# Sketched attention into a top-1 mixture of experts: rows of a tile fetched by a plain transfer on SP's queue, tasks in a new order

## The chip, the cores and the metric

One Trainium2 chip, one of its cores. The metric is the device time of one execution in microseconds (us); lower is better. A core has five engines that run their own instruction queues: TensorE (PE in the profile, with its weight loads as PEld), VectorE (DVE), ScalarE (ACT), GpSimd (POOL) and SyncE (SP). Transfers between memory and SBUF are issued from SP, ACT or POOL.

## The reference

```python
def _attn_ref(q, k, v, S1, S2):            # q, k, v: (4, 4, 1088, 32)
    def phi(x):                            # 64 features of a row
        a = np.einsum('rd,bhsd->bhsr', S1, x)
        b = np.einsum('rd,bhsd->bhsr', S2, x)
        return np.einsum('bhsi,bhsj->bhsij', a, b).reshape(*x.shape[:-1], r * r)
    q_p, k_p = (phi(q), phi(k))
    kv = np.einsum('bhsf,bhsd->bhfd', k_p, v)
    z = np.sum(k_p, axis=2)
    num = np.einsum('bhsf,bhfd->bhsd', q_p, kv)
    den = np.einsum('bhsf,bhf->bhs', q_p, z)[..., None] + 1e-06
    return num / den

def _moe_ref(x, w_gate, w1, w2):           # x: (4352, 128), 8 experts, F = 1024
    logits = x @ w_gate
    expert_idx = np.argmax(logits, axis=1)
    probs = softmax(logits)
    gate_w = probs[np.arange(N), expert_idx]
    for e in range(E):
        mask = expert_idx == e
        out[mask] = gate_w[mask, None] * (np.maximum(x[mask] @ w1[e], 0.0) @ w2[e])
```

The result of the attention, its heads side by side, is the `x` of the mixture: 4352 tokens of 128 numbers, each of which goes through one of eight experts.

## The kernel before

The kernel has two halves that overlap. **Attention** goes by the four batches (`b`) in two chunks of 512 rows (`c`) and a remainder of 64 rows, two batches' remainders together (`r`). Task names in `ORDER` (lines 50 to 58) carry these numbers: `T.Kbc` turns a chunk of keys on PE, `P.Kbc` projects it and makes the features, `V.Kbc` adds to the key-value state, `E.b` and `B.b` finish that state, `T.Q`, `P.Q`, `U.Q`, `N.Q` do the same for queries and divide. A name with `kr` or `qr` is a remainder. `A.b` copies a batch's values beside a column of ones (POOL), `L` issues the last batch's loads and the 16 loads of expert weights (SP).

**Routing** of a batch: `C.b` picks the expert (DVE), `G.b` takes the exponentials (ACT), `R.b` ranks the tokens within their experts with matmuls (PE, DVE), and `S.b` scatters the batch's rows into `xs_dram` in HBM, 128 rows to an indirect transfer of POOL (line 515): 8 or 9 transfers for a batch, 34 in all. An expert has `NTOK` rows of room in `xs_dram`; a row is 128 numbers, the gate weight and the token's number (`XW` = 130 words of 4 bytes).

**Experts** go by tiles of 128 rows of one expert. Up to `JT` = 41 tiles exist: 34 that always run (`JMIN`) and seven more in three optional groups of 4, 2 and 1, which run inside `tc.If` blocks (lines 808 to 821). Which expert and which rows a tile has is worked out by `table()` on DVE: the first table (tasks `W.i`) covers the first ten tiles (`JE`), full tiles of the tokens of batches 0 and 1 alone; the second covers the rest, once batch 3 is ranked, and its steps are called in the loop for tiles 5 and 6 (line 832). A tile goes through:

- `F.j` = `gather(j)` (line 691): an indirect transfer of POOL that fetches 128 rows by a list of 128 row numbers, `grow`, one of each partition; a number out of bounds fetches nothing
- `I.j` = `x_in(j)` (line 700): transpose on PE (line 703), copy on ACT, a register load and a copy of the expert's first weights on DVE (lines 706, 709)
- `Y.j` = `up(j)` (line 720): 16 matmuls (line 724), relu on ACT and DVE
- `Z.j` = `rows_out(j)` and `down(j)` (lines 711, 733): 16 matmuls (line 740), scaling on ACT; the list `to` of the tokens' numbers, of which `inv_i` makes the invalid ones out of bounds
- `store(j)` (line 745): an indirect transfer of POOL that writes 128 rows of the output

`Y` and `Z` are called half tiles in the text below. `ORDER` is written out by hand or by a program ahead of time; under the manual schedule each engine runs its instructions in the order in which the tasks issue them, and semaphores are set by the framework. After `ORDER` a loop (line 794) goes on with tile 5: it turns tile j + 2, does `up` of j + 1 and `down` of j, and then issues gathers `AHEAD` = 6 tiles ahead, one gather of an optional tile while there are any, and stores:

```python
        for i in range(JE, j + AHEAD + 1) if j == 6 else [j + AHEAD] if j > 6 else []:
            if i < JMIN:
                gather(i)
        if j > 6 and optional:
            gather(optional.pop(0))
        for _ in range(0 if j < 6 else j % 2 if optional else 2 if j + 1 < JMIN else JT):
            if waiting:
                store(waiting.pop(0))
```

Gathers rotate through 10 buffers, the optional tiles have seven of their own. Loads of the attention's inputs and of weights are issued on SP's queue from line 154 on, in the order in which they stand.

Of the kernel before, what the change touches and what calls it, by code (L numbers as in the profile page):

```python
# [32 lines left out]
FP = mybir.dt.float32  # L34
# [16 lines left out]
finish_s T.K00 T.K01 P.K00 P.K01 T.K11 T.K10 T.kr0 V.K00 P.kr0 D P.K11 P.K10 T.Q00 T.Q01 L T.Q11  # L51
V.K01 P.Q01 E.0 P.Q00 B.0 P.Q11 T.qr0 U.Q01 U.Q00 T.K21 T.Q10 N.Q00 P.qr0 N.Q01 C.0 P.Q10 P.K21
V.K10 V.K11 T.kr1 G.0 T.K20 R.0 U.qr0 U.Q11 E.1 P.K20 B.1 A.2 U.Q10 T.Q20 N.qr0 N.Q10 N.Q11 V.K20
V.K21 C.1 P.Q20 P.kr1 G.1 T.K31 T.Q21 A.3 R.1 T.K30 W.0 U.Q20 P.Q21 P.K30 P.K31 E.2 W.1 T.Q30 W.2
T.Q31 T.qr1 W.3 U.Q21 S.0 P.Q31 B.2 W.4 P.Q30 V.K30 S.1 N.Q21 N.Q20 V.K31 P.qr1 W.5 F.0 W.6 E.3 C.2
U.Q30 B.3 F.1 F.2 U.qr1 U.Q31 F.3 N.qr1 F.4 N.Q30 G.2 I.0 F.5 N.Q31 I.1 R.2 Y.0 I.2 I.3 C.3 Y.1 Z.0
I.4 Y.2 Z.1 F.6 G.3 S.2a I.5 S.2b R.3 Y.3 Y.4 S.3a S.3b Z.2 F.7 Y.5 Z.3 F.8 Z.4 I.6 F.9
# [4 lines left out]
def kernel(  # L62
# [12 lines left out]
    nc = tc.nc  # L75
# [60 lines left out]
    main = {}  # L136

# [28 lines left out]
    load_rem(lambda b: q_rem[:, b // 2], q, nc.sync, 0)  # L166
    load_main("k", k, 2)
# [284 lines left out]
    xs_dram = dram.tile([E * NTOK, XW], I32, name="xs_dram")  # L452

# [76 lines left out]

    tiles = {}
    done = const.tile([128, E], FP, name="done")

    def table(g, n, j0):
# [30 lines left out]
        if g:  # L565
# [36 lines left out]
        gr = tj("grow", I32, const)  # L602
        iv = None
# [9 lines left out]
        nc.vector.tensor_scalar(loc, loc, 128.0, iota_p, ALU.mult, ALU.add)  # L613
        if g:
# [179 lines left out]
    for j in range(sum(name[0] == "Z" for name in begun), JMIN):  # L794
# [28 lines left out]
        else:  # L823
# [52 lines left out]
```

## Time and profile before

| | us |
|---|---|
| median of 3 runs (283.54 to 286.17) | 283.83 |
| the profiled execution | 284.85 |
| its span in the trace | 282.7 |
| PE busy | 231.8 |
| POOL busy | 134.2 |
| DVE busy | 108.5 |
| ACT busy | 75.4 |

The profiled execution is 2.15 us longer than its span, since something lies around the span. Busy times are sums over instructions; matmuls are pipelined and their ends are modelled, so a busy PE is not PE at its peak. Idle time of an engine is put down to whatever released the next instruction; "issue" means that the profile shows nothing that it waited for. The granted clock (PEclk) is a share of 2.4 GHz.

### The profile page before, as it was taken

The page shows a single profiled execution, that of the slowest core. Times are in us where ns is not written, and L with a number is a line of the kernel's source. Part 1 is how long each engine was busy: PE and PEld are TensorE (multiplying, and loading weights), DVE is VectorE, ACT ScalarE, POOL GpSimd, SP SyncE. Part 2 cuts the span into 40 slices and gives each one's busy share as a digit, 9 for nine tenths or more (in the row PEclk, how much of TensorE's full clock was granted, in tenths as well). Part 3 has the DMA queues.
Part 4 walks back from the last instruction along what each step waited for, and adds up shares of the span by engine and source line. Part 5 has one row for each costly group of instructions (what it writes and reads, how often), then busy time and mean ns, then how long its engine had stood idle before and what let it go on. Part 6 is the DMA issues. An engine that isn't in the chain of part 4 may idle for free.

```text
span 282.7 us, 6720 instructions
## 1 busy us (share of the span) xinstructions
PE 231.8 (82%) x2558; PEld 216.2 (76%) x2558; DVE 108.5 (38%) x303; ACT 75.4 (27%) x198; POOL 134.2 (47%) x165
## 2 busy tenths in 40 slices
PE   8989875957975959669939559887887999999993
PEld 7989764836954949539939349787777998999993
DVE  4656735515844805410641012324323234224320
ACT  2555420404340305013200012221212232333321
POOL 5520373273072564740057747667576156263223
PEclk9999997975996886957977758999997999999999
DMA  6969999211011010110002111111110001010000
GB/s 196 286 191 361 367 377 376 84 47 31 2 40 28 30 48 20 59 38 0 2 21 56 36 38 33 50 35 44 33 48 26 17 21 44 14 37 21 20 9 21
DMA packets 23009, 22.69 MB, mean 80 GB/s; under 512 B 5844, under 2 KB 20184, under 8 KB 22976
## 3 DMA queue, kind: packets, MB, share of 16 engines
q1 hardware_dynamic: 18160, 14.95, 16.3%
q0 software_dynamic: 3712, 7.15, 8.6%
q8 instruction: 23, 0.38, 0.6%
q10 hardware_dynamic: 1104, 0.13, 0.3%
q14 instruction: 10, 0.08, 0.1%
HBM read 17.81 MB, written 4.95 MB: 81 GB/s over the span
## 4 chain that ended last, share of the span: by engine, by line
PE 65%; issue 19%; another core or an unknown queue 6%; ACT 3%; DMA 2%; POOL 2%; DVE 1%; POOLq 1%; ACTq 0%; DVEq 0%
PE ph L724 23%; PE py L740 18%; PE kv L342 4%; PE ab_K L319 4%; PE qp_Q L405 3%; PE nd_Q L417 3%; PE ab_Q L319 3%; PE idle L179 2%; PE tp_Q L310 1%; PE xgTp L703 1%; DMA out_dram<-y,to 1%; PE tp_K L310 1%; ACT q_pT_Q L408 1%; POOL out_dram L747 1%
## 5 line engine op out<-in xcount | busy, mean ns | idle before, releaser
L740 PE MATMUL py<-w_all,hT 128*128 x592 | 81.5, 290 | 9.9 <-issue 6.7
L724 PE MATMUL ph<-xgT,w 128*128 128x128 f32 x592 | 83.6, 295 | 7.3 <-issue 5.2
L724 PEld LDWEIGHTS ph<-xgT,w 128*128 128x128 f32 x592 | 77.7, 209 | 12.1 <-issue 9.9
L740 PEld LDWEIGHTS py<-w_all,hT 128*128 128x128 f32 x592 | 75.9, 205 | 12.8 <-issue 10.1
L692 POOL DMA_INDIRECT x_rows<-xs_dram,grow x41 | 42.9, 1047 | 48.4 <-issue 28.2
L731 DVE TENSOR_SCALAR hT<-ph 128x512 f32<-128x512 f32 x30 | 20.7, 691 | 101.6 <-ACT hT L726 70.0
L747 POOL DMA_INDIRECT out_dram<-y,to x34 | 35.0, 1031 | 43.3 <-ACT xgT L705 28.4
L515 POOL DMA_INDIRECT xs_dram<-x_rows,row_i x34 | 36.3, 1067 | 31.9 <-DVE base_e L509 9.5
L726 ACT ACTIVATE hT<-ph 128x512 f32<-128x512 f32 x37 | 22.2, 599 | 73.2 <-PE ph L724 36.9
L709 DVE COPY w<-w_all 128x1024 f32 x38 | 26.4, 704 | 20.7 <-remote 16.6
L743 ACT ACTIVATE y<-py,x_rows 128x128 f32<-128x128 f32 x34 | 12.5, 368 | 60.3 <-remote 27.6
L417 PE MATMUL nd_Q<-kvx,q_pT_Q 128*64 128x82 f32 x256 | 13.0, 244 | 7.0 <-issue 5.7
L703 PE MATMUL xgTp<-ident,x_rows 128*128 128x128 f32 x38 | 10.5, 298 | 7.8 <-DMA x_rows<-xs_dram,grow 4.4
L417 PEld LDWEIGHTS nd_Q<-kvx,q_pT_Q 128*64 128x64 f32 x256 | 10.8, 141 | 7.6 <-issue 5.6
L319 PE MATMUL ab_K<-s_cat,xT_K 128*64 128x64 f32 x256 | 12.0, 233 | 4.8 <-issue 4.4
L327 DVE TENSOR_TENSOR k_p<-half_K 128x1024 f32<-128x1024 f32 x8 | 10.5, 1328 | 11.7 <-issue 6.1
L319 PEld LDWEIGHTS ab_K<-s_cat,xT_K 128*64 128x64 f32 x256 | 9.7, 144 | 6.7 <-issue 6.3
L705 ACT COPY xgT<-xgTp 128x128 f32<-128x128 f32 x38 | 9.5, 265 | 15.3 <-remote 8.0
L327 DVE TENSOR_TENSOR q_p_Q<-half_Q 128x1024 f32<-128x1024 f32 x8 | 10.4, 1324 | 8.1 <-ACT half_Q L326 8.1
L342 PEld LDWEIGHTS kv<-k_p,v_aug 128*33 128x33 f32 x256 | 9.0, 125 | 4.1 <-issue 4.1
L342 PE MATMUL kv<-k_p,v_aug 128*33 128x64 f32 x256 | 10.4, 239 | 1.9 <-issue 1.9
L703 PEld LDWEIGHTS xgTp<-ident,x_rows 128*128 128x128 f32 x38 | 5.5, 149 | 7.5 <-issue 7.2
(164 smaller groups left out, 193.4 us busy)
## 6 DMA issues: line engine op xcount, KB each, us to landing
w_all<-in_moe_w_dram SPq DMA_DIRECT2D x16, 512.0 KB
k<-in_k_dram SPq DMA_DIRECT2D x4, 512.0 KB
v<-in_v_dram SPq DMA_DIRECT2D x4, 512.0 KB
q<-in_q_dram SPq DMA_DIRECT2D x4, 512.0 KB
x_rows<-xs_dram,grow POOLq DMA_INDIRECT x41
xs_dram<-x_rows,row_i POOLq DMA_INDIRECT x34
out_dram<-y,to POOLq DMA_INDIRECT x34
q_rem<-in_q_dram SPq DMA_DIRECT2D x4, 32.0 KB
```

The lines of the kernel that those rows point to most:

```text
L319: nc.tensor.matmul(ab[ts(m, 64)].rearrange("p (g i r) -> p g i r", g=4, i=n)[:, :, i], lhsT=st["xT"][:, ds(i * 128 + m * 64, 64)], rhs=s_c ...
L327: nc.vector.tensor_tensor(f.rearrange("p g (a b) -> p g a b", a=R), half[:, :, 0:R, None].broadcast_to(shape), half[:, :, None, R:2 * R].b ...
L342: nc.tensor.matmul(kv[b][g * RR:g * RR + DA, ts(n, RR)], lhsT=v1[:, h], rhs=k_p[:, h], start=(first and n == 0), stop=last, skip_group_che ...
L417: nc.tensor.matmul(nd[ts(m, 64), i, ds(hp * 2 * KC, 2 * KC)], lhsT=t[:, ds((i * NP + hp) * 128 + m * 64, 64)], rhs=kvx[bs[m]][:, hp].rearr ...
L515: d = nc.gpsimd.indirect_dma_start(out=xs_dram[:], out_offset=bass.IndirectOffsetOnAxis(ap=row_i[:, u:u + 1], axis=0), in_=x[:, u, :].bitc ...
L692: d = nc.gpsimd.indirect_dma_start(out=xg_of(j).bitcast(I32), out_offset=None, in_=xs_dram[:], in_offset=bass.IndirectOffsetOnAxis(ap=tile ...
L709: nc.vector.tensor_copy(out=w1, in_=w1_all[:, ds(wo, F)])
L724: nc.tensor.matmul(ph[:, ts(c, 128)], lhsT=w1[:, ts(c, 128)], rhs=xT, start=True, stop=True)
L726: nc.scalar.activation(hT[:, 0:512], ph[:, 0:512], AF.Relu)
L731: nc.vector.tensor_scalar(hT[:, 512:1024], ph[:, 512:1024], 0.0, None, ALU.max)
L740: nc.tensor.matmul(py[:, :DM], lhsT=hT[:, ts(c, 128)], rhs=w2_all[:, ds(wo + c * DM, DM)], start=(c == 0), stop=(c == NFC - 1))
L747: d = nc.gpsimd.indirect_dma_start(out=out[:], out_offset=bass.IndirectOffsetOnAxis(ap=to_of(j), axis=0), in_=y, in_offset=None, bounds_ch ...
```

## The change

A tile's rows are taken as 128 consecutive rows from one row number. The number comes out of the table as one value per tile (`first_row`), is loaded into a register of SP, and a plain transfer of SP's queue fetches the rows. An expert's last tile, which would reach past the expert's rows, is shifted back so that it ends with them (`min(of - 128, loc)`), and rows that belong to the tile before are marked invalid for the store, as are rows past the end of an expert with fewer than 128 rows in all. For the latter case the first 128 rows of each expert's room in `xs_dram` are filled with zeros, by one transfer on SP's queue ahead of the loads of batch 2. Optional tiles that don't run get tile numbers beyond the last tile. The tasks stand in a new order, and in the loop up to two stores are issued for each tile from tile 5 on. The declaration of `xs_dram`, of `zeros` and of `parts` moves up.

```diff
 ORDER = """
-finish_s T.K00 T.K01 P.K00 P.K01 T.K11 T.K10 T.kr0 V.K00 P.kr0 D P.K11 P.K10 T.Q00 T.Q01 L T.Q11
-V.K01 P.Q01 E.0 P.Q00 B.0 P.Q11 T.qr0 U.Q01 U.Q00 T.K21 T.Q10 N.Q00 P.qr0 N.Q01 C.0 P.Q10 P.K21
-V.K10 V.K11 T.kr1 G.0 T.K20 R.0 U.qr0 U.Q11 E.1 P.K20 B.1 A.2 U.Q10 T.Q20 N.qr0 N.Q10 N.Q11 V.K20
-V.K21 C.1 P.Q20 P.kr1 G.1 T.K31 T.Q21 A.3 R.1 T.K30 W.0 U.Q20 P.Q21 P.K30 P.K31 E.2 W.1 T.Q30 W.2
-T.Q31 T.qr1 W.3 U.Q21 S.0 P.Q31 B.2 W.4 P.Q30 V.K30 S.1 N.Q21 N.Q20 V.K31 P.qr1 W.5 F.0 W.6 E.3 C.2
-U.Q30 B.3 F.1 F.2 U.qr1 U.Q31 F.3 N.qr1 F.4 N.Q30 G.2 I.0 F.5 N.Q31 I.1 R.2 Y.0 I.2 I.3 C.3 Y.1 Z.0
-I.4 Y.2 Z.1 F.6 G.3 S.2a I.5 S.2b R.3 Y.3 Y.4 S.3a S.3b Z.2 F.7 Y.5 Z.3 F.8 Z.4 I.6 F.9
+finish_s T.K00 T.K01 P.K00 P.K01 T.kr0 T.K11 T.K10 P.kr0 D V.K00 P.K10 P.K11 T.Q01 T.Q00 L T.Q11 V.K01 P.Q00
+E.0 P.Q01 B.0 P.Q11 T.qr0 U.Q00 U.Q01 T.Q10 T.K21 N.Q00 P.qr0 P.Q10 N.Q01 V.K10 C.0 P.K21 G.0 V.K11 U.Q10
+T.K20 T.kr1 R.0 U.Q11 E.1 P.K20 U.qr0 B.1 T.Q20 N.qr0 A.3 N.Q11 N.Q10 C.1 A.2 P.Q20 P.kr1 G.1 V.K20 T.K31
+S.0 T.K30 T.Q21 R.1 W.0 V.K21 U.Q20 P.K31 E.2 P.Q21 W.1 P.K30 B.2 T.Q31 W.2 S.1 W.3 T.Q30 U.Q21 T.qr1 N.Q20
+N.Q21 V.K30 P.qr1 W.4 P.Q30 V.K31 W.5 P.Q31 F.0 E.3 U.qr1 U.Q30 B.3 F.1 F.2 F.3 C.2 G.2 U.Q31 N.Q30 I.0
+N.Q31 I.1 F.4 R.2 F.5 S.2a Y.0 I.2 S.2b F.6 F.7 N.qr1 C.3 I.3 Y.1 G.3 Z.0 Y.2 I.4 Y.3 Z.1 Y.4 R.3 F.8 Z.2
+S.3a I.5 Z.3 Z.4 W.6 S.3b Y.5 F.9 I.6
 """
...
     load_rem(lambda b: q_rem[:, b // 2], q, nc.sync, 0)
+    nc.sync.dma_start(out=xs_dram.rearrange("(e r) c -> r e c", e=E)[0:128],
+                      in_=zeros[:, None, :].bitcast(I32).broadcast_to([128, E, XW]))
     load_main("k", k, 2)
...
             begin = t1("begin", I32)
-            for i, (run, below) in enumerate(((4, 0), (2, 4), (1, 6))):
-                if i:
-                    nc.vector.tensor_scalar(begin[:, i:i + 1], bits[:, 0:1], below, None, ALU.bitwise_and)
+            nc.vector.memset(begin[:, 0:1], 0)
+            for i, below in (1, 4), (2, 6):
+                nc.vector.tensor_scalar(begin[:, i:i + 1], bits[:, 0:1], below, None, ALU.bitwise_and)
...
             begin_f = t1("begin_f")
-            nc.vector.tensor_copy(out=begin_f[:, 1:3], in_=begin[:, 1:3])
+            nc.vector.tensor_scalar(begin_f[:, 0:3], bits, 0, float(JT), ALU.is_equal, ALU.mult)
+            nc.vector.tensor_tensor(begin_f[:, 0:3], begin_f[:, 0:3], begin[:, 0:3], ALU.add)
             jn = tj("jn")
-            nc.vector.tensor_copy(out=jn, in_=jio[:, 0:n])
             base = JMIN - JE
-            nc.vector.tensor_scalar(jn[:, base + 4:base + 6], jio[:, base:base + 2], begin_f[:, 1:2], None, ALU.add)
-            nc.vector.tensor_scalar(jn[:, base + 6:base + 7], jio[:, base:base + 1], begin_f[:, 2:3], None, ALU.add)
+            nc.vector.tensor_copy(out=jn[:, 0:base], in_=jio[:, 0:base])
+            for i, tiles_here in enumerate(parts):
+                a, m = tiles_here[0] - JE, len(tiles_here)
+                nc.vector.tensor_scalar(jn[:, a:a + m], jio[:, base:base + m], begin_f[:, i:i + 1], None, ALU.add)
             yield
...
-        nc.vector.tensor_scalar(loc, loc, 128.0, iota_p, ALU.mult, ALU.add)
+        nc.vector.tensor_scalar(loc, loc, 128.0, None, ALU.mult)
         if g:
...
             nc.vector.tensor_scalar(of, of, cnt[:, 0:1], None, ALU.add)
-            inv = tj("inv")
-            nc.vector.tensor_tensor(inv, loc, of, ALU.is_ge)
+            begin = tj("begin_row")
+            nc.vector.scalar_tensor_tensor(begin, of, -128.0, loc, ALU.add, ALU.min)
+            nc.vector.tensor_scalar(begin, begin, 0.0, None, ALU.max)
+            nc.vector.scalar_tensor_tensor(first, ej, float(NTOK), begin, ALU.mult, ALU.add)
+
+            nc.vector.tensor_scalar(begin, begin, iota_p, None, ALU.add)
+            nc.vector.tensor_tensor(loc, begin, loc, ALU.is_lt)
+            nc.vector.tensor_tensor(begin, begin, of, ALU.is_ge)
+            nc.vector.tensor_tensor(loc, loc, begin, ALU.max)
             iv = tj("inv_i", I32, const)
-            nc.vector.tensor_scalar(iv, inv, float(2 ** 30), None, ALU.mult)
-            nc.vector.scalar_tensor_tensor(loc, ej, float(NTOK), loc, ALU.mult, ALU.add)
-            nc.vector.scalar_tensor_tensor(gr, inv, float(2 ** 22), loc, ALU.mult, ALU.add)
+            nc.vector.tensor_scalar(iv, loc, float(2 ** 30), None, ALU.mult)
         else:
-            nc.vector.scalar_tensor_tensor(gr, ej, float(NTOK), loc, ALU.mult, ALU.add)
+            nc.vector.scalar_tensor_tensor(first, ej, float(NTOK), loc, ALU.mult, ALU.add)
...
     def gather(j):
-        d = nc.gpsimd.indirect_dma_start(
-            out=xg_of(j).bitcast(I32), out_offset=None, in_=xs_dram[:],
-            in_offset=bass.IndirectOffsetOnAxis(ap=tiles[j][1], axis=0),
-            bounds_check=E * NTOK - 1, oob_is_err=False)
+        _, (row,) = nc.values_load_multi_w_load_instructions(
+            tiles[j][1], engines=[mybir.EngineType.SP], min_val=0, max_val=E * NTOK - 128,
+            skip_runtime_bounds_check_because="the table keeps a tile within its expert's rows")
+        d = nc.sync.dma_start(out=xg_of(j).bitcast(I32), in_=xs_dram[ds(row, 128), :])
...
-        for _ in range(0 if j < 6 else j % 2 if optional else 2 if j + 1 < JMIN else JT):
+        for _ in range(2 if j + 1 < JMIN else JT):
             if waiting:
                 store(waiting.pop(0))
```

## Rows read from the trace of the kernel before

**Rows 1.** The page's first part: busy us, share of the span, instructions, by engine.
```profile
PE 231.8 (82%) x2558; PEld 216.2 (76%) x2558; DVE 108.5 (38%) x303; ACT 75.4 (27%) x198; POOL 134.2 (47%) x165
```
**Rows 2.** Stages: length, PE, PEld, DVE, ACT, POOL busy (instructions), PEclk, DMA share, GB/s.
```profile
20.00:40.00 20.00, 17.97 (x386) 16.49 (x383) 13.48 (x31) 9.86 (x25) 7.05 (x7) 1.00 1.04 351
...
130.00:141.40 11.40, 11.39 (x97) 11.19 (x96) 4.34 (x17) 3.32 (x8) 0.00 (x0) 0.95 0.01 1
...
245.00:278.30 33.30, 33.30 (x299) 33.16 (x298) 11.11 (x25) 9.87 (x25) 11.76 (x11) 1.00 0.07 21
```
**Rows 3.** Stages again, cut where PE begins and ends to drip.
```profile
78.30:82.90 4.60, 3.44 (x55) 2.73 (x51) 2.70 (x12) 2.77 (x8) 3.69 (x4) 1.00 0.18 47
82.90:88.40 5.50, 2.00 (x22) 1.30 (x21) 0.00 (x0) 0.00 (x0) 3.32 (x4) 0.85 0.19 48
...
101.40:105.80 4.40, 1.56 (x15) 1.04 (x14) 0.00 (x0) 0.52 (x2) 2.54 (x3) 0.77 0.14 48
109.00:116.60 7.60, 7.60 (x61) 7.52 (x61) 5.28 (x24) 2.17 (x4) 6.06 (x6) 0.89 0.15 47
116.60:126.30 9.70, 4.17 (x13) 2.63 (x12) 0.28 (x2) 0.37 (x1) 6.07 (x7) 0.72 0.16 48
...
143.00:155.80 12.80, 9.78 (x61) 9.62 (x61) 3.01 (x8) 0.86 (x2) 10.06 (x10) 0.73 0.17 43
155.80:168.80 13.00, 6.99 (x22) 4.91 (x22) 0.85 (x2) 1.23 (x3) 8.16 (x9) 0.60 0.15 40
...
187.00:189.10 2.10, 1.30 (x12) 1.22 (x11) 0.00 (x0) 0.00 (x0) 0.98 (x1) 1.00 0.20 62
...
199.20:201.40 2.20, 0.95 (x6) 0.64 (x5) 0.00 (x0) 0.00 (x0) 1.00 (x1) 1.00 0.21 60
...
209.90:213.40 3.50, 1.34 (x7) 0.82 (x6) 1.97 (x4) 0.97 (x3) 1.94 (x2) 0.95 0.13 36
```
**Rows 4.** Instructions in time, within a drip: start, us, engine, line, [idle before].
```profile
161.44 1.00 POOL L692 DMA_INDIRECT x_rows<-xs_dram,grow  x1 [0.30 <-issue]
161.56 0.37 PE L724 MATMUL ph<-xgT,w 128*128 128x128 f32 x1
...
162.26 0.37 PE L724 MATMUL ph<-xgT,w 128*128 128x128 f32 x1 [0.33 <-issue]
```
**Rows 5.** Instructions in time: half tiles behind three drips, and one late in the kernel.
```profile
90.73 3.37 PE L724 MATMUL ph<-xgT,w 128*128 128x128 f32 x16 [0.52 <-DVE den_Q L422]
...
169.06 3.40 PE L740 MATMUL py<-w_all,hT 128*128 x16
...
213.45 3.47 PE L740 MATMUL py<-w_all,hT 128*128 x16 [1.62 <-ACT y L743]
...
256.31 1.95 PE L740 MATMUL py<-w_all,hT 128*128 x16
```
**Rows 6.** Groups by line: count, busy us and mean ns of one, idle before.
```profile
L692 POOL DMA_INDIRECT x_rows<-xs_dram,grow x41 | 42.9, 1047 | 48.4 <-issue 28.2
```
**Rows 7.** Instructions in time: the second table's end, tile 10's gather, two late transposes.
```profile
142.03 0.19 DVE L628 SCALAR_TENSOR_TENSOR grow<-inv,loc 128x31 int32<-128x31 f32 x1
...
142.97 1.11 POOL L692 DMA_INDIRECT x_rows<-xs_dram,grow  x1 [18.47 <-issue]
...
145.76 0.45 PE L703 MATMUL xgTp<-ident,x_rows 128*128 128x128 f32 x1 [4.37 <-DMA x_rows<-xs_dram,grow]
...
195.54 0.30 PE L703 MATMUL xgTp<-ident,x_rows 128*128 128x128 f32 x1 [1.81 <-DMA out_dram<-y,to]
```
**Rows 8.** Two lines' instructions: ns min/median/max, first and last start in us.
```profile
L706 DVEq TENSOR_LOAD <-woff x38: 299/304/547, 89.0 to 268.3; - x38
...
L140 SPq DMA_DIRECT2D k<-in_k_dram x4: 396/528/615, 1.2 to 19.6; - x4
```
**Rows 9.** Queue of program code (packets, MB, share), 183 to 184 and 230 to 282 us.
```profile
q8 instruction: 1, 0.02, 8.1%
...
q8 instruction: 4, 0.07, 0.5%
```

More of the change, by code (lines that the diff above doesn't have):

```diff
@@ L136 @@
     main = {}
+    xs_dram = dram.tile([E * NTOK, XW], I32, name="xs_dram")
+    zeros = const.tile([128, XW], FP, name="zeros")
+    nc.vector.memset(zeros, 0.0)
     def load_main(name, src, b):
@@ L172 @@
     load_main("q", q, 2)
-    zeros = const.tile([128, 128], FP, name="zeros")
-    nc.vector.memset(zeros, 0.0)
     idle = bank_ps("idle")
     for i in range(12):
-        nc.tensor.matmul(idle[:, 0:128], lhsT=zeros, rhs=zeros, start=True, stop=True)
+        nc.tensor.matmul(idle[:, 0:128], lhsT=zeros[:, 0:128], rhs=zeros[:, 0:128], start=True, stop=True)
     ident = const.tile([128, 128], FP, name="ident")
@@ L449, in query_rem @@
               lambda: rows_of(2 * r + 1, J, 1))
-    xs_dram = dram.tile([E * NTOK, XW], I32, name="xs_dram")
     def route(b):
@@ L526, in route @@
         task[f"S.{b}a"], task[f"S.{b}b"] = lambda: scatter(range(J // 2 + n - J)), lambda: scatter(range(J // 2 + n - J, n))
+    parts = [range(JMIN, JMIN + 4), range(JMIN + 4, JMIN + 6), range(JMIN + 6, JMIN + 7)]
     tiles = {}
@@ L601, in table @@
         yield
-        gr = tj("grow", I32, const)
-        iv = None
+        first, iv = tj("first_row", I32, const), None
         if g:
@@ L622, in table @@
             nc.vector.tensor_scalar(of, of, cnt[:, 0:1], None, ALU.add)
-            inv = tj("inv")
-            nc.vector.tensor_tensor(inv, loc, of, ALU.is_ge)
+            begin = tj("begin_row")
[6 more added lines that the diff above has]
+            nc.vector.tensor_tensor(loc, loc, begin, ALU.max)
             iv = tj("inv_i", I32, const)
-            nc.vector.tensor_scalar(iv, inv, float(2 ** 30), None, ALU.mult)
-            nc.vector.scalar_tensor_tensor(loc, ej, float(NTOK), loc, ALU.mult, ALU.add)
-            nc.vector.scalar_tensor_tensor(gr, inv, float(2 ** 22), loc, ALU.mult, ALU.add)
+            nc.vector.tensor_scalar(iv, loc, float(2 ** 30), None, ALU.mult)
         else:
-            nc.vector.scalar_tensor_tensor(gr, ej, float(NTOK), loc, ALU.mult, ALU.add)
+            nc.vector.scalar_tensor_tensor(first, ej, float(NTOK), loc, ALU.mult, ALU.add)
         for j in range(n):
-            tiles[j0 + j] = (wo[0:1, j:j + 1], gr[:, j:j + 1], None if iv is None else iv[:, j:j + 1])
+            tiles[j0 + j] = (wo[0:1, j:j + 1], first[0:1, j:j + 1], None if iv is None else iv[:, j:j + 1])
         if not g:
@@ L640, in table @@
             nc.vector.tensor_tensor(done, nt, before, ALU.min)
-    parts = [range(JMIN, JMIN + 4), range(JMIN + 4, JMIN + 6), range(JMIN + 6, JMIN + 7)]
     after = {16: 0, 20: 1, 24: 2}
```

## The prediction

> **What bounds the kernel now.** I read the busy times first: TensorE (PE) is busy for 231.8 of 282.7 us [rows 1], so it sets the end, and the question is what its idle and slow time consists of. The table of stages then shows two kinds of stretch. In the last 33 us PE is never idle and a matmul takes 33.30 / 299 = 0.111 us; the same holds from 130 to 141.4 us [rows 2]. Elsewhere it drips: from 155.8 to 168.8 us it got through 22 matmuls in 13.0 us, from 116.6 to 126.3 us through 13 in 9.7 us [rows 3]. A close look shows single matmuls 0.7 us apart, put down to "issue", so the profile knows of nothing that PE waits for [rows 4].
>
> The drips stand beside work of GpSimd (POOL). Each comes in pairs of stretches [rows 3]: first POOL issues indirect transfers back to back (0.30 us between them [rows 4]) and PE runs, then, 5 to 13 us into such a run, PE drips, until POOL pauses (two earlier drips, from 40.6 and 55.7 us, are of the kind of the one at 101.4 us, behind scatters alone; the one at 55.7 us begins 1.7 us after its run). Where POOL is idle (130 to 141.4 us) or issues one transfer per tile (11 in the last 33 us) there is none [rows 2]. This is a coincidence in time, nine times over, not a shown cause. After a drip the next half tile (16 matmuls) is slow: 3.37, 3.40 and 3.47 us where one takes 1.95 us late in the kernel [rows 5]; the granted clock in the drip stretches fell as low as 0.60 [rows 3], and 0.5 would be the 1.2 GHz level.
>
> What fills the runs: seven gathers from 78.3 to 88.4 us (a call across the cut counts on both sides), nine scatters and three gathers from 109 us, gathers with stores from 143 to 168.8 us [rows 3]. 41 gathers hold POOL for 42.9 us [rows 6].
>
> **The change, part by part.** I sum against the profiled execution (284.85 us, a span of 282.7 and 2.15 around it) and take off 1.0 at the end, since the median of the three runs shown is 283.83.
>
> *Gathers leave POOL.* 41 calls go (42.9 us [rows 6], and 0.30 us of gap each). What this takes away by stage:
> (a) The run of gathers at 78.3 to 88.4 us goes whole. Its drip is 5.5 us with 2.00 us of PE work, so 3.5 idle; its matmuls are smaller than a tile's and were stretched too, so I take 4.0. The slow half tile behind it costs 3.37 - 1.95 = 1.4 [rows 3, 5]. Gain 5.4.
> (b) The scatters stay. The drip at 101.4 to 105.8 us belongs to a run of scatters alone; I leave it. The run from 109 us loses its three gathers; now the waiting stores of tiles 0 to 5 come straight behind the nine. Three to six calls of 1.3 us make a run as long as before or 3.7 us longer. Loss 0 to 3.7; I take 1.0, because a store waits for its tile's result, and a dripping PE delivers that late, which breaks the run.
> (c) From 143 us POOL has only stores. A store can start when its tile is done, so it goes at the pace of the tiles, one per 3.7 us, the pattern of the last 33 us [rows 2]. The drip of 13.0 us held 22 x 0.111 = 2.4 us of work: 10.6 back, and 3.40 - 1.95 = 1.4 for the slow half behind it [rows 3, 5]. Gain 12.0.
> (d) The short drips at 187, 199.2 and 209.9 us lose 2.1 - 1.3 = 0.8, 2.2 - 0.7 = 1.5 and 3.5 - 0.8 = 2.7 us, the slow half at 213.45 us another 1.5 [rows 3, 5]; together 6.5. Some of it may belong to the conditional blocks of lines 808 to 821, for which no row stands alone: between 0 and 6.5. I keep 2.0 for them and count 4.5. The transpose at 195.54 us waited 1.81 us [rows 7] for a transfer behind a crowded POOL; a gather on SP is issued six tiles ahead without that crowd: 1.8. Gain 6.3.
>
> *Gather on SP's queue.* Each needs a register load on SP (0.30 us, the price of the same load on VectorE) and an issue (0.40 to 0.62 us, 512 KB loads) [rows 8]. So 0.7 to 0.92 us of a queue that has nothing else to do once the weights are issued; for ten gathers in a row 9 us, against 1.3 us each on POOL. Only two places see the latency: tile 0, behind the first table, and tile 10, behind the second. For tile 10 the row number was ready at 142.22 us, POOL began at 142.97, and PE transposed at 145.76: 3.5 us from table to PE, after which PE was late [rows 7]. By the new way: 0.7 to 0.92 plus what follows POOL's 1.11 us (1.7 us), 2.4 to 2.6; or, if the plain transfer itself is as slow as the whole old call (2.8), up to 3.7. I take 2.9: gain 0.6, bounds -0.2 to 1.1. Tile 0 counts the same in kind; its cover is the work of attention that PE has left, so nothing. What SP's wait blocks is only later gathers, each six tiles ahead (22 us); if that cover were gone, each would cost some 3 us.
>
> *The zeros.* 128 rows of each expert's 520 bytes are written once, 0.53 MB on SP's queue ahead of the third batch's loads; at the 351 GB/s of the full stretch [rows 2] that delays them 1.5 us. The weights behind them are wanted only at 90.7 us [rows 5]; cost nothing, 1.5 us if the third batch's keys have no slack. The scatters now wait for this write too, which is issued some 20 us ahead of the first of them.
>
> *The tables.* About seven small VectorE operations are added, most behind the row number; one of them at this width takes 0.19 us [rows 7]. The row number itself comes out one operation earlier. VectorE is idle around there; cost nothing, 1.3 us if not.
>
> *The new order.* The routing work of the third and fourth batch moves by one or two half tiles (1.95 us each [rows 5]); the two early drips stay, since their scatters stay. I take 0 and bound it at -3.6 to 3.6.
>
> Sum: 5.4 - 1.0 + 12.0 + 6.3 + 0.6 = 23.3. 284.85 - 23.3 = 261.6, and 260.5 on the scale of the median.
>
> A rule speaks against most of this. The Trainium skill, "DMA: Bandwidth & Descriptors", section "Issuing engines are not separate DMA queues", says that transfers of all engines run on the same 16 DMA engines, and that another issuing engine saves only the issue time, usually small. By that alone the change is worth the waits for data, 1.8 + 0.6 = 2.4 us, so 281.4. The trace does not bear it out yet: from 20 to 40 us SP's loads filled the DMA engines (351 GB/s) and PE was busy for 17.97 of 20 us [rows 2], so the issuer seems to matter.
>
> **The rivals.** *First, the drips are not POOL's.* A long program arrives piece by piece (queue q8, 0.02 MB each, by their number PE's), and a piece sometimes lands a few us before a drip, as the one at 183 us does before that at 187 us [rows 9]. Then the drips stay, and the gain is the waits of (d) and of tile 10: 2.4 us, 281.4. Against it: four pieces landed after 230 us [rows 9] without a drip, and every drip ends when POOL pauses. 0.10. The Trainium skill, "Runtime: NRT & Kernel Launch", section "Instruction fetch mechanics", counts sequential fetch as hidden, which agrees with those four pieces.
>
> *Second, the drips move to the stores.* Stores come earlier now (from tile 5 on, two per tile), so the scatter run grows into them and the stretch of (c) keeps a drip. Then (c) and 4.5 of (d) are lost: 23.3 - 16.5 = 6.8 us gained, 277; with half of (c) back, 271. For it: stores cost POOL as much as gathers. Against it: without gathers POOL has one call per tile. 0.18.
>
> *Third, slower: SP's queue becomes the bound.* If a gather holds SP until it has landed (a wait for the one before), 31 late gathers must fit in the 27 remaining tiles of 3.7 us, 3.2 us each. To eat the whole gain each must take 3.2 + 23.3 / 31 = 4.0 us; at 4.2 us the time is 283.8 - 23.3 + 31 x 1.0 = 291.5. Against it: SP issued whole 512 KB loads every 0.4 to 0.6 us [rows 8], and even a full old gather is 2.8 us. 0.08, other ways of being slower included.
>
> **How the numbers follow.** The forecast has 0.64: 260, its own range 247 (the 12.8 us from 143 us, which held 61 matmuls or 6.8 us of work [rows 3], lose their 6 us too, and the loss of 8.3 us in the drip at 116.6 us, 9.7 - 13 x 0.111, comes down by the most of it) to 268 (bounds of order, zeros and (b) against it). The second rival reaches to 277, so the range is 247 to 277. Measurements of this kernel tell about 1% (2.8 us) from no change. Faster: 0.64 + 0.18 = 0.82; within 1%: 0.10; slower 0.08.
>
> **What would show it.** In the changed kernel's trace POOL has 75 indirect transfers instead of 116, and PE's stretch from its first expert tile has no drip except behind the scatters of the third and fourth batch; PE's first tile starts 5 us earlier. If PE still waits for nothing shown while POOL issues one store per tile, the first rival is right; if drips follow dense stores, the second. If transposes of tiles wait for gathers, the third. The forecast fails outright if the drip needs SP's or any small transfers in HBM rather than POOL's own calls.

## The result, and the profile after

The changed kernel takes 263.58 us (median of 4 runs, 261.88 to 266.94) against 284.64 us for the kernel before, measured beside it: a ratio of 0.9237, 95% interval 0.9157 to 0.9317. The ratio is of fast executions alone; the one of 266.94 us is counted as slow and stands in the median only. The forecast was 260, its range 247 to 277. The profiled execution took 264.15 us, with a span of 261.5 (before 282.7), so 21.2 us of span were gained where the sum said 23.3.

First the page of the kernel after: the busy time by engine, then the two large groups of POOL's transfers (line, engine, operation, count; busy us and mean ns; idle before).

```profile
PE 215.5 (82%) x2558; PEld 206.0 (79%) x2558; DVE 108.9 (42%) x310; ACT 76.0 (29%) x198; POOL 86.1 (33%) x124
...
L757 POOL DMA_INDIRECT out_dram<-y,to x34 | 34.1, 1002 | 92.7 <-ACT xgT L715 68.9
...
L517 POOL DMA_INDIRECT xs_dram<-x_rows,row_i x34 | 34.8, 1023 | 49.4 <-DVE base_e L511 25.3
```

POOL has 124 instructions instead of 165, the 41 gathers [rows 6] gone, and is busy for 86.1 instead of 134.2 us. PE executes the same 2,558 matmuls in 16.3 us less busy time [rows 1]: by the profile's busy times the gain is mostly a PE that no longer crawls, not one that waits less.

Now stages of the kernel after (columns as in [rows 2]): the stretch in which the kernel before had its longest drip [rows 3], and the one in which the kernel after loses most.

```profile
150.00:160.00 10.00, 10.00 (x92) 10.00 (x91) 3.62 (x8) 3.20 (x8) 2.06 (x3) 1.00 0.37 88
...
116.30:127.40 11.10, 0.00 (x0) 0.00 (x0) 0.76 (x2) 1.46 (x5) 6.65 (x7) 0.61 0.11 42
```

From 150 to 160 us PE gets through 92 matmuls in 10 us at the full clock; before, 22 in 13 us [rows 3]. But from 116.3 to 127.4 us not one matmul starts. The instructions in time of the kernel after show what lies around it (start, us, engine, line, tile, [idle before and what ended it]):

```profile
107.49 0.97 POOL L517 DMA_INDIRECT xs_dram<-x_rows,row_i  x1 [6.22 <-DVE to L726]
...
122.88 0.97 POOL L757 DMA_INDIRECT out_dram<-y,to  x1 [0.30 <-issue]
126.58 1.05 POOL L757 DMA_INDIRECT out_dram<-y,to  x1 [2.73 <-ACT y L753]
...
125.94 0.37 ACT L753 ACTIVATE y<-py,x_rows 128x128 f32<-128x128 f32 x1 [12.36 <-remote]
126.10 0.69 DVE L719 COPY w<-w_all 128x1024 f32 x1 [10.80 <-remote]
127.48 3.78 PE L734 MATMUL ph<-xgT,w 128*128 128x128 f32 x16 [11.19 <-ACT xgT L715]
```

Between 107.49 and 123.85 us POOL issues 13 transfers back to back: nine scatters, then four stores. ScalarE stands still for 12.36 us, VectorE for 10.80 (in the middle of the second table), and PE waits 11.19 us behind ScalarE. ScalarE and VectorE go on some 2 us after POOL has paused, PE 1.5 us behind them. The half tile behind it takes 3.78 us where 1.95 is usual.

Two more places of the kernel after: the first up half tile, and tile 10 behind the second table.

```profile
87.69 2.02 PE L734 MATMUL ph<-xgT,w 128*128 128x128 f32 x16 [0.29 <-DVE den_Q L426]
...
141.43 0.19 DVE L634 SCALAR_TENSOR_TENSOR first_row<-ej,begin_row 128x31 int32<-128x31 f32 x1
142.25 3.93 SPq L705 DMA_DIRECT2D x_rows<-xs_dram  x5
144.22 0.30 PE L713 MATMUL xgTp<-ident,x_rows 128*128 128x128 f32 x1 [3.22 <-DMA x_rows<-xs_dram]
144.35 2.01 PE L734 MATMUL ph<-xgT,w 128*128 128x128 f32 x16
```

The first half tile starts 3.0 us earlier than before [rows 5], tile 10's transpose only 1.5 us earlier [rows 7], the end 21.2 us earlier. So two thirds of a sum that should have gained 5 us by tile 10 did not arrive there, and everything behind tile 10 did.

### The profile page after: what moved, and what is told of

Same layout as the page of the kernel before. It is cut to its first block, busy times and chain, and to the rows that moved or that the text cites. A ratio compares the mean times of both kernels' runs of the same rounds, so it can differ in the third digit from the quotient of the medians.

```text
span 261.5 us, 6873 instructions
## 1 busy us (share of the span) xinstructions
PE 215.5 (82%) x2558; PEld 206.0 (79%) x2558; DVE 108.9 (42%) x310; ACT 76.0 (29%) x198; POOL 86.1 (33%) x124
## 5 line engine op out<-in xcount | busy, mean ns | idle before, releaser
L734 PE MATMUL ph<-xgT,w 128*128 128x128 f32 x592 | 75.0, 280 | 13.9 <-ACT xgT L715 11.2
L734 PEld LDWEIGHTS ph<-xgT,w 128*128 128x128 f32 x592 | 71.0, 195 | 15.6 <-ACT xgT L715 12.4
L750 PE MATMUL py<-w_all,hT 128*128 x592 | 73.2, 277 | 1.1 <-issue 1.1
L750 PEld LDWEIGHTS py<-w_all,hT 128*128 128x128 f32 x592 | 69.8, 194 | 1.8 <-issue 1.8
L757 POOL DMA_INDIRECT out_dram<-y,to x34 | 34.1, 1002 | 92.7 <-ACT xgT L715 68.9
L517 POOL DMA_INDIRECT xs_dram<-x_rows,row_i x34 | 34.8, 1023 | 49.4 <-DVE base_e L511 25.3
L323 PE MATMUL ab_Q<-s_cat,xT_Q 128*64 128x64 f32 x256 | 11.8, 235 | 5.7 <-issue 5.7
L323 PEld LDWEIGHTS ab_Q<-s_cat,xT_Q 128*64 128x64 f32 x256 | 9.8, 146 | 6.9 <-issue 6.8
L323 PE MATMUL ab_K<-s_cat,xT_K 128*64 128x64 f32 x256 | 11.2, 236 | 2.3 <-issue 2.0
L409 PE MATMUL qp_Q<-ident,q_p_Q 128*128 128x128 f32 x64 | 10.2, 317 | 0.0
```

The lines of the kernel that those rows point to most:

```text
L323: nc.tensor.matmul(ab[ts(m, 64)].rearrange("p (g i r) -> p g i r", g=4, i=n)[:, :, i], lhsT=st["xT"][:, ds(i * 128 + m * 64, 64)], rhs=s_c ...
L517: d = nc.gpsimd.indirect_dma_start(out=xs_dram[:], out_offset=bass.IndirectOffsetOnAxis(ap=row_i[:, u:u + 1], axis=0), in_=x[:, u, :].bitc ...
L734: nc.tensor.matmul(ph[:, ts(c, 128)], lhsT=w1[:, ts(c, 128)], rhs=xT, start=True, stop=True)
L750: nc.tensor.matmul(py[:, :DM], lhsT=hT[:, ts(c, 128)], rhs=w2_all[:, ds(wo + c * DM, DM)], start=(c == 0), stop=(c == NFC - 1))
L757: d = nc.gpsimd.indirect_dma_start(out=out[:], out_offset=bass.IndirectOffsetOnAxis(ap=to_of(j), axis=0), in_=y, in_offset=None, bounds_ch ...
```

## The experiments

All are compared with the kernel before, run beside them on the same chip; e3 and e5 were executed once each and are read from their traces alone. My theory: POOL's indirect transfers, when they follow each other without a pause, hold up the other engines. Rivals: the new order made the gain; program code or any small transfer is the cause; a busy POOL as such.

**e1 and e2: the two halves of the change.** e1 is the kernel before with the new order alone, e2 the kernel after with the order and the store rule of before.

```diff
# e1, on the kernel before
 ORDER = """ ...the new order... """
-        for _ in range(0 if j < 6 else j % 2 if optional else 2 if j + 1 < JMIN else JT):
+        for _ in range(2 if j + 1 < JMIN else JT):
# e2, on the kernel after: the same two places, from new to old
```

> The kernel before with the new order of the tasks and the new rule for stores; gathers stay on POOL as indirect transfers. Theory 1 (the drips of PE come with POOL's back-to-back indirect transfers, and the gain is that gathers left POOL): the drips behind the first seven gathers and behind gathers mixed with stores stay, so 282 to 290 us, a ratio of 0.99 to 1.02. Rival (the new order carries the gain): 262 to 272 us. Of the early slip of 3 to 4 us that the changed kernel shows ahead of 40 us, this run tells whether the order brings it (then it is here too) or the write of zeros (then it is not).

> The changed kernel with the old order of the tasks and the old rule for stores: plain gathers on SP's queue, zeros and tables alone. Theory 1: 258 to 267 us, the whole gain. Rival (order carries the gain): above 276 us. With the old rule stores start after tile 6, one or two for each tile, so the run of scatters of batch 3 is nine transfers instead of thirteen: theory 1 expects the stall that in the changed kernel lasts from 116.3 to 127.5 us to be some 4 us shorter.

Measured: e1 286.78 us, ratio 1.0158 (1.0064 to 1.0252), with one of its four executions at 420.45 us, for a reason that nothing on record shows; e2 259.95 us, ratio 0.9246 (0.9162 to 0.9330). A stage of e1, with the gathers still on POOL:

```profile
156.00:169.00 13.00, 8.39 (x49) 7.25 (x48) 1.56 (x3) 1.16 (x4) 9.03 (x9) 0.75 0.19 52
```

49 matmuls in 13 us with nine POOL transfers: the drip is there. So the plain gathers carry the whole gain, and at the end the order has none that these runs can tell. One part of my expectation missed: with the old store rule too, four stores followed batch 3's nine scatters at once in e2 (105.36 to 122.5 us), so the rule doesn't decide how long that run is.

On the way the order does show. The first up half tile and tile 10's transpose, in e1 and then in e2:

```profile
87.86 3.40 PE L724 MATMUL ph<-xgT,w 128*128 128x128 f32 x16 [0.27 <-DVE den_Q L422]
148.93 0.45 PE L703 MATMUL xgTp<-ident,x_rows 128*128 128x128 f32 x1 [4.41 <-DMA x_rows<-xs_dram,grow]
```

```profile
88.24 2.02 PE L734 MATMUL ph<-xgT,w 128*128 128x128 f32 x16 [0.29 <-DVE den_Q L426]
140.10 0.30 PE L713 MATMUL xgTp<-ident,x_rows 128*128 128x128 f32 x1 [3.16 <-DMA x_rows<-xs_dram]
```

With the gathers on POOL the new order starts the first half tile 2.9 us earlier (90.73 before [rows 5]) and makes the stretch from there to tile 10 6.0 us longer (61.07 us in e1, 55.03 before). With the gathers on SP it starts it 0.6 us earlier and makes that stretch 4.7 us longer (56.53 us in the kernel after, 51.86 in e2). These are single profiled executions, and they scatter: e3 and e5, whose code up to there is that of the kernel after, reach tile 10 at 149.65 and 146.64 us instead of 144.22. That the order loses there fits e7 and e8 below (39.7 us from the first half tile to tile 10 with the new order, 37.7 with the old), but it isn't shown.

**e3: a pulse of each suspect.** Extra work at three quiet places of the kernel after: 12 indirect transfers of POOL behind tile 9, 12 plain ones of SP behind tile 25, 12 fills of POOL (no transfer) behind tile 29.

```diff
+        if j == 9:
+            nc.gpsimd.iota(idx, ..., base=0, channel_multiplier=1, ...)
+            for i in range(12):
+                d = nc.gpsimd.indirect_dma_start(out=scr[:], ...idx[:, i:i + 1]..., in_=zeros...)
...
+        if j == 25:
+            for i in range(24, 36):
+                nc.sync.dma_start(out=scr[ts(i, 128), :], in_=zeros...)
+        if j == 29:
+            for i in range(12):
+                nc.gpsimd.memset(spare, 0.0)
```

> The changed kernel with three pulses of extra work put into its clean stretch, where PE does a tile in 3.68 us: 12 indirect transfers of POOL back to back behind tile 9 (128 rows of 520 bytes of zeros into a spare tensor in HBM), 12 plain transfers of the same size on SP's queue behind tile 25, and 12 fills of 128 x 1024 on POOL (about 1 us each) behind tile 29. Theory 1: PE loses 6 to 12 us within the first pulse and under 1 us in each of the others; some 271 to 276 us in all. Rival A (drips belong to places in the program, not to POOL): no pulse costs anything, 263 to 265 us. Rival B (small transfers in HBM, whoever issues them): the second pulse costs as much as the first, 280 us. Rival C (a busy POOL, whatever it does): the third costs as much.

Stages of e3, one for each pulse:

```profile
162.60:181.10 18.50, 11.74 (x53) 9.41 (x52) 2.20 (x5) 2.35 (x6) 11.41 (x12) 0.65 0.21 62
227.90:240.00 12.10, 12.10 (x111) 12.10 (x110) 4.67 (x10) 3.87 (x10) 2.76 (x3) 1.00 0.38 99
260.60:272.00 11.40, 11.07 (x100) 10.88 (x98) 3.13 (x7) 3.34 (x8) 10.83 (x11) 1.00 0.02 7
```

In the first 18.5 us PE got through 53 matmuls; at 0.111 us each that is 5.9 us of work, so 12.6 us are lost. The plain transfers of SP, more bytes per second (99 GB/s), cost nothing, and neither does a POOL that is busy for 10.83 of 11.40 us with fills. Its instructions in time show the delay with which the drip begins:

```profile
159.37 0.99 POOL L860 DMA_INDIRECT scr<-zeros,idx  x1 [0.28 <-POOL idx L858]
...
164.36 0.51 PE L753 MATMUL py<-w_all,hT 128*128 x3 [0.29 <-issue]
...
173.82 0.99 POOL L860 DMA_INDIRECT scr<-zeros,idx  x1 [0.30 <-issue]
...
178.01 3.13 PE L753 MATMUL py<-w_all,hT 128*128 x13 [0.34 <-issue]
```

The first matmul behind a gap comes 5.0 us after the run begins, and the drip ends 1.9 us after the run does (a store follows the twelfth transfer, to 176.09 us). The drip is made here at a place where the kernel after has none: that the order made the gain is rejected once more. So is, for this drip, a late piece of PE's program: no packet of q8 lands between 158 and 181 us, and PE goes on without one. (The execution took 287.81 us where I expected 271 to 276, some 24 more than the kernel after: 12.6 in this pulse, 5.4 by tile 10, ahead of all pulses (149.65 against 144.22 us), and some 5 at the end, where the last four stores began only at 273.25 us, behind the fills.)

**e5: indirect, or issued by POOL? close together, or many?** Behind tile 9 the 12 transfers of POOL are plain ones; behind tile 25 POOL issues 8 indirect ones with a fill between them.

```diff
+        if j == 9:
+            for i in range(24, 36):
+                nc.gpsimd.dma_start(out=scr[ts(i, 128), :], in_=zeros...)
+        if j == 25:
+            nc.gpsimd.iota(idx, ...)                              # as in e3
+            for i in range(8):
+                d = nc.gpsimd.indirect_dma_start(out=scr[:], ...idx[:, i:i + 1]..., in_=zeros...)
...
+                nc.gpsimd.memset(spare, 0.0)
```

> The kernel after, with two stretches of extra work on POOL. Behind tile 9 POOL issues 12 plain transfers (128 rows of 520 bytes to a scratch area, no indices); behind tile 25 it issues 8 indirect transfers of the same size with a fill of 128x1024 (0.97 us) between any two. If indirect transfers as such slow TensorE, the plain run costs nothing (half tiles stay near 1.95 us) and the spaced run costs some 3 to 8 us. If it is transfers that POOL issues close together, whatever their addresses, the plain run costs some 6 to 13 us, as the 12 indirect ones of e3_pulse did, and the spaced run costs under 1 us. If the plain ones are issued faster or slower than one per 1.27 us, the loss goes with the rate.

Stages of e5 around the two pulses, and the plain pulse itself among the instructions in time:

```profile
157.50:176.00 18.50, 18.50 (x168) 18.50 (x167) 7.52 (x16) 5.88 (x16) 11.79 (x18) 1.00 0.33 90
231.40:250.00 18.60, 18.60 (x169) 18.60 (x169) 9.90 (x15) 5.61 (x15) 17.00 (x18) 1.00 0.11 35
```

```profile
157.53 6.61 POOL L859 DMA_DIRECT2D scr<-zeros  x12
```

Both stretches are clean: 168 and 169 matmuls at the full clock. The plain run lasts longer than the 5.0 us after which the drip of e3 began, and two stores follow it at once, so POOL issues 14 transfers in 9.4 us. The indirect transfers of both pulses write 128 consecutive rows each, as the plain ones do, since `idx` is filled that way; and both kinds share the queue q0, with 32 packets for each transfer of POOL on the page of the kernel after (75 transfers) and of e5 (95):

```profile
q0 software_dynamic: 2400, 4.50, 4.9%
```

```profile
q0 software_dynamic: 3040, 5.83, 6.4%
```

Neither theory had it whole. Plain transfers of POOL do no harm, even at one per 0.55 us; and indirect ones do none when one comes per 2.1 to 2.4 us. What hurts is indirect transfers close together. The execution as a whole took 274.14 us, but none of that is lost in the pulses: tile 10's transpose came 2.4 us later than in the kernel after (146.64 us) and the next 1.7 more, ahead of both; and behind the second pulse, which had held the stores up, six of them ran back to back (249.68 to 257 us), whereupon ScalarE stood still for 6.12 us and PE waited 3.60. That loss came beside a dense run once more.

**e6: the zeros.** In the kernel after PE is idle for 2.35 us at 19.4 to 21.7 us, in e2 for 2.06, in e1 and before it isn't. e1 has the new order without the zeros, e2 the zeros without the new order, so the zeros are the suspect. e6 leaves the write out (no tile of this data reads those zeros, since each expert has 128 rows or more).

```diff
-    nc.sync.dma_start(out=xs_dram.rearrange("(e r) c -> r e c", e=E)[0:128],
-                      in_=zeros[:, None, :].bitcast(I32).broadcast_to([128, E, XW]))
```

> The kernel after without the write of zeros to the first 128 rows of every expert (in this data every expert has 128 rows or more, so no tile reads one). If the 1024 packets of the zeros hold up TensorE's program piece and the loads of batch 2, the idle 2.35 us of TensorE at 19.37 to 21.72 go, the first up half tile starts 2 to 3 us before 87.7, and the time is some 261 us. If the new order makes that gap, it stays and the time is that of the kernel after, 263.6.

PE's instructions in time, e2 first (with zeros), then e6 (without):

```profile
21.16 0.81 PE L323 MATMUL ab_Q<-s_cat,xT_Q 128*64 128x64 f32 x21 [2.06 <-issue]
```

```profile
19.13 1.13 PE L321 MATMUL ab_Q<-s_cat,xT_Q 128*64 128x64 f32 x32
20.19 0.33 PE L312 MATMUL tp_qr<-ident,q_rem 128*128 128x128 f32 x1
```

The gap goes, and the first up half tile starts at 85.7 us, 2.0 before that of the kernel after, as expected (in the profiled execution, which with 265.09 us was the longest of the four). At the end nothing of it can be told: 262.80 us, ratio 0.9166 (0.9101 to 0.9230), an interval that overlaps with that of the kernel after. So the write costs 2 us where it stands, and no gain at the end is shown from leaving it out.

**e4, e7, e11, e9: spacing the transfers that stay.** If the cause is indirect transfers close together, a pause between the scatters must help though it makes POOL's work longer. The pause is a fill of unused memory.

```diff
# e4: in scatter(), ahead of each of the 34
+                nc.gpsimd.memset(spare, 0.0)                      # 128x1024
# e7: smaller ahead of the scatters, and ahead of the early stores; zeros behind batch 2's loads
+                nc.gpsimd.memset(spare[:, 0:512], 0.0)
+        if j < 10:                                                # in store(j)
+            nc.gpsimd.memset(spare[:, 0:1024], 0.0)
# e11: as e7, with 0:256 and 0:512
# e9: kernel after; 0:512 ahead of batch 3's nine scatters, 0:1024 ahead of stores 0 to 9, no more
```

> The changed kernel with a fill of 128 x 1024 on POOL (about 1 us) ahead of each of the 34 scatters, so that scatters come every 2.4 us instead of every 1.27. Theory 1 in the form that it is the density of indirect transfers: the stalls behind the four runs of scatters shrink from about 30 us in all to under 10; the last scatter of batch 1 ends some 10 us later in its run, which lies near the first gather, so part is given back: 245 to 256 us. If the number of transfers counts and not their spacing: stalls as long as before or longer, 263 to 272 us.

> The kernel after, with a fill of 128x512 on POOL (some 0.5 us) ahead of each of the 34 scatters, one of 128x1024 (0.97 us) ahead of each of the stores of tiles 0 to 9, and the zeros written behind the loads of batch 2. If it is the spacing that counts and 1.8 us per scatter is enough, gather 0 comes in time (the 10.33 us that TensorE waited at 77.30 in e4_paced_scatters fall under 4), no drip is left and the time is 238 to 244 us. If 1.8 us is too dense, half tiles of 3 to 5 us come back behind S.1 and S.3, and it is 248 to 258.

> e7_paced2 with half as large fills: 128x256 (some 0.3 us) ahead of each scatter and 128x512 ahead of the stores of tiles 0 to 9, so one transfer per some 1.55 us and 1.8 us. If the pause alone counts, however short, tile 10's gather comes 17 x 0.27 = 4.6 us sooner behind batch 2's and 3's scatters and the time falls to some 232 to 235 us. If there is a rate above which TensorE starves between one per 1.27 us and one per 1.68 us, half tiles of over 2.1 us come back and it lies between e7_paced2 and the kernel after, 240 to 258 us.

> The kernel after with fills on POOL only from batch 3's scatters on: 128x512 ahead of each of its nine scatters and 128x1024 ahead of the stores of tiles 0 to 9. The run of 13 back-to-back transfers at 107.5 to 123.9 us is opened; everything ahead of it is as in the kernel after. If that run is what held TensorE from 116.3 to 127.5 us, the stretch comes back but for the wait for tile 10's gather, which now stands behind nine scatters at 1.8 us instead of 1.27 (5 us later): the time is some 252 to 257 us, 7 to 11 less than after. If the engines stand still there for another reason, the idle 11 us stay and the time is 262 or more.

| | one scatter per | us (median) | ratio to before (95%) |
|---|---|---|---|
| after | 1.27 us | 263.58 | 0.9237 (0.9157 to 0.9317) |
| e9 | 1.27, batch 3: 1.68 | 254.49 | 0.8935 (0.8845 to 0.9025) |
| e4 | 2.1 to 3.0 | 248.21 | 0.8814 (0.8742 to 0.8886) |
| e11 | 1.46 | 241.56 | 0.8442 (0.8343 to 0.8542) |
| e7 | 1.68 | 237.74 | 0.8290 (0.8227 to 0.8352) |

The stage of e9 that answers to the standstill of the kernel after (116.3 to 127.4 us above), of the same length:

```profile
115.40:126.50 11.10, 11.10 (x98) 11.01 (x98) 7.98 (x24) 3.44 (x9) 10.17 (x12) 1.00 0.11 37
```

98 matmuls instead of none, with POOL busier than before (10.17 us with its fills). Only the spacing differs there, so the standstill is the run's. The time, 254.49 us, lies in the 252 to 257 expected, and the end gains 9.1 us. Tile 10 waits 5.14 us for its rows, 1.9 more than in the kernel after. I had expected it to wait for the scatters, which take longer now, but the last of them ends at 123.33 us and the row number is ready only at 129.20. What takes longer is the second table, as e9's instructions in time show, and behind them one operation of the same table in the kernel after:

```profile
127.50 1.04 DVE L633 TENSOR_SCALAR of_cnt<-of_cnt,cnt 128x31 f32<-128x31 f32 x1
127.52 0.97 POOL L761 MEMSET spare<- 128x1024 f32 x1
...
129.01 0.19 DVE L637 SCALAR_TENSOR_TENSOR first_row<-ej,begin_row 128x31 int32<-128x31 f32 x1
129.24 1.39 DVE L639 TENSOR_SCALAR begin_row<-begin_row,iota_p 128x31 f32<-128x31 f32 x1
129.63 0.97 POOL L761 MEMSET spare<- 128x1024 f32 x1
...
131.75 0.45 PE L716 MATMUL xgTp<-ident,x_rows 128*128 128x128 f32 x1 [5.14 <-DMA x_rows<-xs_dram]
```

```profile
140.72 0.24 DVE L630 TENSOR_SCALAR of_cnt<-of_cnt,cnt 128x31 f32<-128x31 f32 x1
```

Three TENSOR_SCALAR operations of VectorE that meet a fill of POOL last until the fill ends: 1.35, 1.04 and 1.39 us where the kernel after needs 0.18, 0.24 and 0.24 (a TENSOR_TENSOR amid another fill, at 123.68 us, takes its 0.42 as ever). The first two stand ahead of the row number, and the last part of the table up to it takes 6.7 us instead of 4.8. So a pause made of a fill has a price of its own on VectorE. The wait for the last scatter is what e4 paid for its long pauses, as its instructions in time show for tile 0 (the last scatter ends at 73.93 us, the gather is issued at 75.44):

```profile
77.30 0.47 PE L715 MATMUL xgTp<-ident,x_rows 128*128 128x128 f32 x1 [10.33 <-DMA x_rows<-xs_dram]
```

e7, with shorter pauses, has none for tile 0 and 5.12 us for tile 10, its largest, and there too the last scatter (107.12 us) is done well ahead of the row number (110.89); at 237.74 us it is the shortest of these. (It has the zeros behind batch 2's loads too, worth no more than e6's 2 us.) Of e11, PE's instructions in time behind batch 0's scatters at one per 1.46 us:

```profile
44.77 0.39 PE L422 MATMUL nd_Q<-kvx,q_pT_Q 128*64 128x82 f32 x4 [0.36 <-issue]
45.50 0.42 PE L422 MATMUL nd_Q<-kvx,q_pT_Q 128*64 128x82 f32 x5 [0.34 <-issue]
46.23 0.37 PE L422 MATMUL nd_Q<-kvx,q_pT_Q 128*64 128x82 f32 x3 [0.31 <-issue]
```

Drips are back, so a pause as such is not enough. One transfer per 1.46 us is still too dense; one per 1.68 us leaves single gaps under half a us among e7's scatters.

**e8: e7 with the old order.**

```diff
# e7, with
 ORDER = """ ...the order of the kernel before... """
```

> e7_paced2 with the order of tasks of the kernel before. If the order is worth nothing by itself, it comes within 3 us of e7_paced2; if the new order's earlier scatters are what it has, it is later than e7_paced2 by the wait for gather 0.

237.08 us, ratio 0.8306 (0.8249 to 0.8362): the same as e7. The order is worth nothing in this setting either.

**e10: did the gathers have to move at all?** The kernel before, gathers on POOL, with a fill of 128x512 ahead of every scatter, gather and store.

```diff
# on the kernel before, ahead of each of the three kinds of indirect transfer
+        nc.gpsimd.memset(spare[:, 0:512], 0.0)
```

> The kernel before, with its gathers on POOL as they were and its own order, and a fill of 128x512 (some 0.55 us) ahead of every scatter, gather and store on POOL. If spacing alone takes the drips away, those of rows 3 go (12.0 for 155.8 to 168.8, about 4 for 78 to 88, 4 to 6 for the short ones and some 8 for 116.6 to 126.3) and the gathers' waits grow (POOL then needs 3.6 us for a gather and a store with their fills, against 3.7 us per tile on TensorE, so it has no slack): 255 to 268 us. If the gathers have to leave POOL for the gain, because two transfers per tile on one queue are too many whatever their spacing, it stays at 278 us or more.

266.05 us, ratio 0.9338 (0.9257 to 0.9419). Spacing alone gives about what the change gave. Its largest wait, and who waited for the gathers (us, times):

```profile
112.60 0.45 PE L706 MATMUL xgTp<-ident,x_rows 128*128 128x128 f32 x1 [17.54 <-DMA x_rows<-xs_dram,grow]
```

```profile
  PE xgTp L706: 32.3, 10
```

The drips are gone and PE now waits 32.3 us for gathers that queue on POOL behind paced transfers. e7 and e10 differ by 28.3 us (with the zeros' place and the spacing of the stores in it): the move to SP is worth more once the transfers are spaced than it was by itself.

## Why the prediction was right, step by step

The direction, the size (263.58 against 260) and the mechanism held: POOL's runs slow PE, and taking the gathers out of them gives the time back. Until e3 this was a coincidence in time; e3, e5 and e9 show it. The wording was too wide in one point: I spoke of POOL's own calls and took it that the issuer seems to matter. Plain calls of POOL do no harm; it is indirect ones close together that do. And the sum came out this well behind tile 10 alone: of 5.0 us by tile 10 only 1.5 came, for which two terms that I had put at 0 are the likeliest reasons, the zeros and the new order.

*(a), 5.4 us: right with the old order.* In e2 the drip goes, the half tile behind it takes 2.02 us, and the first half tile starts 2.5 us earlier although the zeros cost PE 2.06 there: some 4.5 against 4.0 for the drip. The 3.0 us of the kernel after are not gathers alone, since e1 starts 2.9 us earlier with its gathers still on POOL.

*The zeros, 0: the step that failed first.* I priced them by their bytes on SP's queue, 1.5 us against the slack of the loads. What they cost lies elsewhere: a piece of PE's program landed at 19 to 20 us in the kernel after, at 17 to 18 before, and PE was idle for 2.35 us. That the piece was late because of this write fits e1, e2 and e6; that it alone held PE is argued, not shown.

*(b), a loss of 1.0: not more, as far as e2 tells.* From the first half tile to tile 10 the sum asked for 1.0 us less than before (slow half tile 1.4 and tile 10 0.6 gained, 1.0 lost); it took 144.22 - 87.69 = 56.53 us against 145.76 - 90.73 = 55.03 [rows 5, 7], 1.5 us more. But e2, with the old order and the same run of 13 calls, took 51.86, 3.2 us less. The stores did fill the run up to 13 calls. My reason for the smaller value, that a dripping PE delivers stores late, was wrong: four stores were ready. I priced the longer run alone; what the whole run costs e9 shows, with 9.1 us at the end.

*Tile 10, 0.6: right.* From the row number (141.62 us) to the transpose it is 2.6 us; I took 2.9, before it was 3.5.

*(c) and (d), 12.0 + 6.3: right.* Behind tile 10 the kernel after takes 261.5 - 144.22 = 117.3 us, before 282.7 - 145.76 = 136.9; of the 19.6 us, 1.6 belong to the half tile behind tile 10 (2.01 us now, 3.63 then), so 18.0 stand against 18.3. In e2 it is 257.4 - 140.10 = 117.3 us as well. PE's idle times behind tile 10 are 1.42, 0.41, 0.35 and 0.33 us, all put down to "issue"; that fits the 2.0 us kept for the conditional blocks, but no run takes it apart.

*The order, 0: right at the end, not on the way.* At the end none of e1, e2 and e8 shows a gain; the loss that e1 shows (ratio 1.0158) is in neither of the others (e2 0.9246 against 0.9237, e8 0.8306 against 0.8290). Tile 10, though, came 3.2 us later in e1 than in the kernel before, and 4.1 later in the kernel after than in e2, about my bound of 3.6. In e2, with the zeros and the old order, 5.7 us had been gained by tile 10, more than the 5.0 of the sum, so the order would account for all that did not arrive. By single executions that is likely, not shown, and why the order should lose there stays open.

*The rivals.* That the drips aren't POOL's (281.4) is rejected by e3, which makes one, and in which no piece of program lands. The Trainium skill's rule ("DMA: Bandwidth & Descriptors", section "Issuing engines are not separate DMA queues") says that another issuing engine saves only the time of the issue. By that alone the change was worth 2.4 us, and it gave 21 of 284.6. For the issuer the trace agrees with the rule: in e5 and e3 twelve plain transfers cost nothing, from POOL as from SP. What the rule doesn't speak of is the kind: the change also made 41 indirect transfers plain, and indirect ones close together hold up engines that issue nothing. That the drips move to the stores came true in one place, the run behind batch 3, and not in the stretch of (c). SP's queue never became the bound: a gather's issue took 0.33 us (median of 41), and PE waited for a gather once, 3.22 us at tile 10.

## What to carry to other kernels

Where TensorE's matmuls stand single with "issue" between them, look at what POOL does at that time: here a run of indirect transfers without pauses cost TensorE, ScalarE and VectorE time, and not only its own queue. Take out of the run what has consecutive rows (a plain transfer with its row number in a register), and space the rest: fills of 0.55 us ahead of the scatters and of 0.97 ahead of the first ten stores made POOL's work longer and the kernel some 10% shorter (263.58 to 237.74 us). Space no more than needed: whoever reads behind the last transfer waits for the sum of the pauses (10.33 us for e4's tile 0), and some operations of VectorE that met a fill lasted until its end.

## What the runs showed of the hardware that was not expected

Twelve indirect transfers of POOL, one per 1.27 us, cost TensorE 12.6 us of an 18.5 us stretch in which the DMA engines were busy for 0.21 of the time; twelve plain ones of POOL, one per 0.55 us, cost nothing with 0.33, and twelve of SP nothing with 0.38. ScalarE and VectorE stop too (12.36 and 10.80 us in the kernel after), and the engines go on about 2 us after the last call. At one call per 1.46 us short drips are left, at 1.68 us single gaps. At one per 2.1 to 2.4 us e5 has none; e4 still has two, of 0.76 and 1.51 us, at scatters that took 1.66 and 1.86 us instead of 0.97. What it is that the engines lack in that time stays open: the profile says "issue" or "remote", and no run here takes the two apart. In e3 it was no piece of PE's program, since none landed.
